# Forgetting attention followed by a SwiGLU block on one core: wider attention blocks, the decay inside the matmul, and the two stages interleaved

## The chip, the cores and the metric

The kernel runs on one core of a Trainium2 chip. The metric is the time of one execution on the device in microseconds. "The profile" is a record of one execution: which engine ran which instruction when, and what it had waited for. PE is the tensor engine, PEld its weight loads, ACT the scalar engine, DVE the vector engine, POOL GpSimd, SP the queue that issues most transfers.

## The reference

There are 64 heads (8 batches of 8 heads), 576 positions of 64 numbers each. The rows of attention are then the 4608 tokens of a gated feed-forward block (FFN) of width 512 and inner width 1536.

```python
scores = scale * q @ k.transpose(0, 1, 3, 2)
cum = cumsum(log(clip(f, 1e-4, 1)), axis=-1)
scores = where(causal, -1e9, scores + cum[:, :, :, None] - cum[:, :, None, :])
attn = softmax(scores) @ v                    # 64 heads, 576 x 576, causal
x = attn.transpose(0, 2, 1, 3).reshape(4608, 512)
g = x @ w_gate                                # 512 x 1536
out = (g * sigmoid(g) * (x @ w_val)) @ w_out  # 1536 x 512
```

## The kernel before

Attention comes first, head by head, in blocks of 96 by 96. q and k are transposed on PE in pieces of 96 by 64, so scores contract over 64 rows.

```python
for bh in range(BH):
    ...                                   # q, k, v by GpSimd transfers, cast to bf16
    for c in range(NBLK):                 # 6 blocks of 96
        nc.tensor.transpose(tq, qn[:, c, :], idN)
        nc.scalar.activation(qTp[:, c * BLK : (c + 1) * BLK], tq, AF.Copy, scale=scale)
        nc.tensor.transpose(tk, kn[:, c, :], idN)
        nc.vector.tensor_copy(kTp[:, c * BLK : (c + 1) * BLK], tk)
    ...                                   # cum_bc: decay of the queries on all rows
    for qi in range(NBLK):
        for kj in range(qi + 1):
            nc.tensor.matmul(sp, kTp[:, kj block], qTp[:, qi block])
            nc.vector.tensor_add(spa, sp, cum_bc[:, qi block])
            nc.scalar.activation(pt, spa, AF.Exp, bias=ncum_col[:, kj : kj + 1])
            ...                           # kj == qi: times a triangle, on DVE
            nc.tensor.matmul(op, pt, vb[:, kj, :], start=(kj == 0), stop=(kj == qi))
        ...                               # divide by the sum, store to attn_x in DRAM
```

Only when all heads are stored are the FFN's weights loaded. The FFN then takes 9 tiles of 512 tokens; each loads its rows from DRAM, transposes them on PE and does 144 matmuls of 512 columns.

The softmax here doesn't subtract the row's maximum and nothing guards it: scores larger than these inputs give would overflow.

Of the kernel before, what the change touches and what calls it, by code (L numbers as in the profile page):

```python
# [8 lines left out]
F32 = mybir.dt.float32  # L9
BF16 = mybir.dt.bfloat16  # L10
AF = mybir.ActivationFunctionType


@with_exitstack
def kernel(
    ctx: ExitStack,
    tc: tile.TileContext,
    q: bass.AP,
    k: bass.AP,
    v: bass.AP,  # L20
    f: bass.AP,
    moe_w_gate: bass.AP,
    moe_w_val: bass.AP,
    moe_w_out: bass.AP,
    out: bass.AP,
):
    nc = tc.nc
    B, H, S, D = q.shape
    BH = B * H
    N_TOK, D_MODEL = out.shape  # L30
    D_FF = moe_w_gate.shape[1]
    assert D_MODEL == H * D
    scale = 1.0 / (D ** 0.5)

    BLK = 96
    NBLK = S // BLK
    assert NBLK * BLK == S

    x_dram = nc.dram_tensor("attn_x", (N_TOK, D_MODEL), F32, kind="Internal").ap()
    cum_dram = nc.dram_tensor("cum_f", (BH, S), F32, kind="Internal").ap()  # L40
    ncum_dram = nc.dram_tensor("ncum_f", (BH, S), F32, kind="Internal").ap()

    fflat = f.rearrange("b h s -> (b h) s")
# [4 lines left out]
    with tc.tile_pool(name="cum", bufs=1) as cp:  # L48
        lf = cp.tile([BH, S], F32)
        nc.sync.dma_start(out=lf, in_=fflat)  # L50
        nc.scalar.activation(lf, lf, AF.Ln)
        tmp = cp.tile([BH, S], F32)
        d = 1
        src = lf
        dst = tmp
        while d < S:
            nc.vector.tensor_copy(dst[:, :d], src[:, :d])
            nc.vector.tensor_add(dst[:, d:], src[:, d:], src[:, : S - d])  # L58
            src, dst = dst, src
            d *= 2  # L60
        nc.sync.dma_start(out=cum_dram, in_=src)
        nc.scalar.mul(dst, src, -1.0)
        nc.sync.dma_start(out=ncum_dram, in_=dst)

    consts = ctx.enter_context(tc.tile_pool(name="consts", bufs=1))
    tri = consts.tile([BLK, BLK], F32)
    make_upper_triangular(nc, tri[:, :], val=1.0, diag=True)
    idN = consts.tile([BLK, BLK], BF16)
    make_identity(nc, idN[:, :])

    with ExitStack() as actx:
        hp = actx.enter_context(tc.tile_pool(name="head", bufs=2))
        pp = actx.enter_context(tc.tile_pool(name="p", bufs=3))
        psum = actx.enter_context(tc.tile_pool(name="psum", bufs=3, space=bass.MemoryType.PSUM))
        opsum = actx.enter_context(tc.tile_pool(name="opsum", bufs=2, space=bass.MemoryType.PSUM))
        tpsum = actx.enter_context(tc.tile_pool(name="tpsum", bufs=1, space=bass.MemoryType.PSUM))

        for bh in range(BH):
            b = bh // H
            h = bh % H  # L80
            qn = hp.tile([BLK, NBLK, D], BF16)
            kn = hp.tile([BLK, NBLK, D], BF16)
            nc.gpsimd.dma_start(out=qn, in_=qf[bh].rearrange("(n p) d -> p n d", p=BLK))  # L83
            nc.gpsimd.dma_start(out=kn, in_=kf[bh].rearrange("(n p) d -> p n d", p=BLK))  # L84
            qTp = hp.tile([D, S], BF16)
            kTp = hp.tile([D, S], BF16)
            for c in range(NBLK):
                tq = tpsum.tile([D, BLK], BF16)
                nc.tensor.transpose(tq, qn[:, c, :], idN)  # L89
                nc.scalar.activation(qTp[:, c * BLK : (c + 1) * BLK], tq, AF.Copy,  # L90
                                     scale=scale)
                tk = tpsum.tile([D, BLK], BF16)
                nc.tensor.transpose(tk, kn[:, c, :], idN)  # L93
                nc.vector.tensor_copy(kTp[:, c * BLK : (c + 1) * BLK], tk)  # L94
            cum_bc = hp.tile([BLK, S], F32)
            nc.gpsimd.dma_start(out=cum_bc[:1, :], in_=cum_dram[bh : bh + 1, :])
            nc.gpsimd.partition_broadcast(cum_bc, cum_bc[:1, :])
            ncum_col = hp.tile([BLK, NBLK], F32)
            nc.gpsimd.dma_start(
                out=ncum_col, in_=ncum_dram[bh].rearrange("(n p) -> p n", p=BLK)  # L100
            )
            vb = hp.tile([BLK, NBLK, D + 1], BF16)
            nc.gpsimd.dma_start(
                out=vb[:, :, :D], in_=vf[bh].rearrange("(n p) d -> p n d", p=BLK)
            )
            nc.vector.memset(vb[:, :, D : D + 1], 1.0)

            for qi in range(NBLK):
                op = opsum.tile([BLK, D + 1], F32)
                for kj in range(qi + 1):  # L110
                    sp = psum.tile([BLK, BLK], F32)
                    nc.tensor.matmul(  # L112
                        sp,
                        kTp[:, kj * BLK : (kj + 1) * BLK],
                        qTp[:, qi * BLK : (qi + 1) * BLK],
                        start=True,
                        stop=True,
                    )
                    spa = pp.tile([BLK, BLK], F32)
                    nc.vector.tensor_add(spa, sp, cum_bc[:, qi * BLK : (qi + 1) * BLK])  # L120
                    pt = pp.tile([BLK, BLK], BF16)
                    if kj == qi:
                        ptf = pp.tile([BLK, BLK], F32)
                        nc.scalar.activation(ptf, spa, AF.Exp,  # L124
                                             bias=ncum_col[:, kj : kj + 1])
                        nc.vector.tensor_mul(pt, ptf, tri)  # L126
                    else:
                        nc.scalar.activation(pt, spa, AF.Exp,  # L128
                                             bias=ncum_col[:, kj : kj + 1])
                    nc.tensor.matmul(  # L130
                        op, pt, vb[:, kj, :], start=(kj == 0), stop=(kj == qi)
                    )
                recip = pp.tile([BLK, 1], F32)
                nc.vector.reciprocal(recip, op[:, D : D + 1])  # L134
                ot = pp.tile([BLK, D], F32)
                nc.scalar.activation(ot, op[:, :D], AF.Copy, scale=recip)  # L136
                nc.sync.dma_start(
                    out=x_dram[b * S + qi * BLK : b * S + (qi + 1) * BLK,
                               h * D : (h + 1) * D],
                    in_=ot,  # L140
                )

    P = 128
    MT = 512
    KD = D_MODEL // P
    KF = D_FF // P

    idP = consts.tile([P, P], BF16)
    make_identity(nc, idP[:, :])

    wpool = ctx.enter_context(tc.tile_pool(name="wpool", bufs=1))
    wg = wpool.tile([P, KD, D_FF], BF16)
    wv = wpool.tile([P, KD, D_FF], BF16)
    wo = wpool.tile([P, KF, D_MODEL], BF16)
    nc.gpsimd.dma_start(out=wg, in_=moe_w_gate.rearrange("(ko p) n -> p ko n", p=P))
    nc.gpsimd.dma_start(out=wv, in_=moe_w_val.rearrange("(ko p) n -> p ko n", p=P))
    nc.gpsimd.dma_start(out=wo, in_=moe_w_out.rearrange("(ko p) n -> p ko n", p=P))

    xp = ctx.enter_context(tc.tile_pool(name="xp", bufs=2))
    xtp = ctx.enter_context(tc.tile_pool(name="xtp", bufs=2))  # L160
    hpool = ctx.enter_context(tc.tile_pool(name="hp2", bufs=2))
    spool = ctx.enter_context(tc.tile_pool(name="sp2", bufs=3))
    fpsum = ctx.enter_context(tc.tile_pool(name="fpsum", bufs=2, space=bass.MemoryType.PSUM))
    ops = ctx.enter_context(tc.tile_pool(name="ops", bufs=2, space=bass.MemoryType.PSUM))
    tps2 = ctx.enter_context(tc.tile_pool(name="tps2", bufs=2, space=bass.MemoryType.PSUM))
    opool = ctx.enter_context(tc.tile_pool(name="opool", bufs=3))

    NMT = N_TOK // MT
    for mt in range(NMT):
        xt = xtp.tile([P, KD, MT], BF16)  # L170
        for ms in range(MT // P):
            xn = xp.tile([P, D_MODEL], BF16)
            nc.gpsimd.dma_start(  # L173
                out=xn, in_=x_dram[mt * MT + ms * P : mt * MT + (ms + 1) * P, :]
            )
            for ko in range(KD):
                tp = tps2.tile([P, P], BF16)
                nc.tensor.transpose(tp, xn[:, ko * P : (ko + 1) * P], idP)  # L178
                nc.vector.tensor_copy(xt[:, ko, ms * P : (ms + 1) * P], tp)  # L179
# [59 lines left out]
```

## Time and profile before

| | before |
|---|---|
| median of the first 5 runs | 1107.03 us (1106.3 to 1109.13) |
| busy: PE, ACT, DVE, POOL | 93%, 56%, 53%, 27% |
| attention, to about 740 us | 11.0 us a head |
| FFN, from about 770 us | about 39 us a tile |

The lines from which these come are shown in the prediction. A high busy share says only that some instruction was in the array; how many columns pass per microsecond has to be read from start to start.

### The profile page before, as it was taken

The numbers are of one execution on the slowest core, as the hardware profiler recorded it, in microseconds if no ns is written. First come the engines' busy times: TensorE is split into PE (matmuls) and PEld (weight loads), VectorE is DVE, ScalarE is ACT, GpSimd is POOL, SyncE is SP. The second block draws the span as 40 slices with busy tenths as digits, with TensorE's granted clock in tenths as the row PEclk, the third lists the DMA queues.
The fourth block names the chain that finished last, engine by engine and source line by source line (L and its number), as shares of the span: only waits on it lengthen the run. The fifth ranks groups of instructions, "written<-read, shape, count | busy, mean of one in ns | idle before, by whom it ended". The sixth has DMA issues, their size and how long they took to land.

```text
span 1104.2 us, 18439 instructions
## 1 busy us (share of the span) xinstructions
PE 1022.5 (93%) x4896; PEld 608.3 (55%) x4896; DVE 581.9 (53%) x2868; ACT 618.8 (56%) x2225; POOL 299.4 (27%) x433
## 2 busy tenths in 40 slices
PE   0899999999999999999999999977989889889888
PEld 0566666666666666666666666642434334334333
DVE  2566666666666666666666666652333333333333
ACT  1677777777777777777777777752112112202211
POOL 1443434343433333333343333320000000000000
PEclk9999999999999999999999999999999899889899
DMA  1543534343434444444444444338110220120111
GB/s 21 37 36 35 46 34 37 33 38 33 37 33 37 35 35 36 34 35 35 36 35 36 35 35 35 30 53 163 48 49 19 49 57 20 39 58 29 29 48 39
DMA packets 174090, 44.43 MB, mean 40 GB/s; under 512 B 162016, under 2 KB 168160, under 8 KB 173984
## 3 DMA queue, kind: packets, MB, share of 16 engines
q0 software_dynamic: 125552, 23.91, 27.3%
q1 hardware_dynamic: 48432, 19.34, 7.4%
q8 instruction: 38, 0.62, 0.2%
q14 instruction: 68, 0.56, 0.2%
HBM read 47.63 MB, written 19.17 MB: 60 GB/s over the span
## 4 chain that ended last, share of the span: by engine, by line
PE 72%; issue 19%; DMA 6%; DVE 1%; POOL 1%; ACT 0%; POOLq 0%; ACTq 0%
PE sp L112 26%; PE op L130 23%; PE tk L93 7%; PE tq L89 6%; DMA xn<-attn_x 5%; PE gp L185 3%; PE vp L190 3%; PE op L200 3%; PE tp L178 1%; DMA qn<-in_q_dram 0%; DVE xt L179 0%; DVE tmp L58 0%; DVE lf L58 0%; DMA lf<-in_f_dram 0%; DMA attn_x<-ot 0%
## 5 line engine op out<-in xcount | busy, mean ns | idle before, releaser
L112 PE MATMUL sp<-qTp,kTp 64*96 64x96 bf16 x1344 | 373.0, 306 | 1.9 <-DVE spa L120 1.9
L128 ACT ACTIVATE pt<-spa,ncum_col 96x96 bf16<-96x96 f32 x960 | 326.7, 367 | 47.0 <-PE op L130 39.9
L130 PE MATMUL op<-vb,pt 96*96 96x65 bf16 x1344 | 334.6, 285 | 0.4 <-ACT pt L128 0.2
L120 DVE TENSOR_TENSOR spa<-sp,cum_bc 96x96 f32<-96x96 f32 x1344 | 297.6, 244 | 19.0 <-ACT pt L128 14.3
L130 PEld LDWEIGHTS <-pt 96*96 96x96 bf16 x1344 | 188.2, 161 | 102.9 <-DVE pt L126 1.3
L112 PEld LDWEIGHTS <-kTp 64*96 64x96 bf16 x1344 | 190.2, 158 | 80.9 <-issue 3.2
L195 ACT ACTIVATE st<-gp 128x512 f32<-128x512 f32 x108 | 64.4, 597 | 271.0 <-PE gp L185 270.9
L124 ACT ACTIVATE ptf<-spa,ncum_col 96x96 f32<-96x96 f32 x384 | 139.8, 364 | 26.5 <-DVE spa L120 26.5
L196 DVE TENSOR_TENSOR hh<-st,vp 128x512 bf16<-128x512 f32 x108 | 74.3, 688 | 142.0 <-PE vp L190 142.0
L134 DVE RECIPROCAL recip<-op 96x1 f32<-96x1 f32 x384 | 62.9, 164 | 157.3 <-PE op L130 150.6
L89 PE MATMUL tq<-idN,qn 96*64 96x96 bf16 x384 | 108.8, 283 | 28.5 <-POOL idN masks.py:199 24.7
L185 PE MATMUL gp<-xt,wg 128*128 128x512 bf16 x432 | 123.6, 410 | 9.5 <-DMA wg<-in_moe_w_gate_dram 9.2
L136 ACT ACTIVATE ot<-op,recip 96x64 f32<-96x64 f32 x384 | 115.4, 301 | 29.5 <-DVE recip L134 24.6
L90 ACT ACTIVATE qTp<-tq 64x96 bf16<-64x96 bf16 x384 | 90.5, 236 | 70.5 <-PE tq L89 70.5
L94 DVE COPY kTp<-tk 64x96 bf16<-64x96 bf16 x384 | 75.3, 196 | 92.8 <-PE tk L93 92.5
L190 PE MATMUL vp<-xt,wv 128*128 128x512 bf16 x432 | 116.1, 393 | 1.9 <-DMA wv<-in_moe_w_val_dram 1.9
L93 PE MATMUL tk<-idN,kn 96*64 96x96 bf16 x384 | 110.0, 287 | 1.3 <-DVE kTp L94 0.9
L173 POOL DMA_DIRECT2D xn<-attn_x x36 | 19.2, 535 | 323.1 <-PE tp L178 316.9
L126 DVE TENSOR_TENSOR pt<-ptf,tri 96x96 bf16<-96x96 f32 x384 | 96.2, 250 | 3.2
L200 PE MATMUL op<-wo,hh 128*128 128x512 bf16 x432 | 94.7, 379 | 0.0
L83 POOL DMA_DIRECT2D qn<-in_q_dram x64 | 46.7, 729 | 173.5 <-PE op L130 155.2
L84 POOL DMA_DIRECT2D kn<-in_k_dram x64 | 46.8, 731 | 137.6 <-PE op L130 128.7
(36 smaller groups left out, 527.4 us busy)
## 6 DMA issues: line engine op xcount, KB each, us to landing
attn_x<-ot SPq DMA_DIRECT2D x384, 24.0 KB, 1.4
out_dram<-ot SPq DMA_DIRECT2D x36, 256.0 KB, 2.0
qn<-in_q_dram POOLq DMA_DIRECT2D x64, 72.0 KB, 2.9
kn<-in_k_dram POOLq DMA_DIRECT2D x64, 72.0 KB, 2.7
vb<-in_v_dram POOLq DMA_DIRECT2D x64, 72.0 KB, 2.9
xn<-attn_x POOLq DMA_DIRECT2D x36, 128.0 KB, 3.0
wg<-in_moe_w_gate_dram POOLq DMA_DIRECT2D x1, 1536.0 KB, 10.5
wv<-in_moe_w_val_dram POOLq DMA_DIRECT2D x1, 1536.0 KB, 17.2
```

Of the source, the lines that this page charges most:

```text
L89: nc.tensor.transpose(tq, qn[:, c, :], idN)
L93: nc.tensor.transpose(tk, kn[:, c, :], idN)
L112: nc.tensor.matmul(sp, kTp[:, kj * BLK : (kj + 1) * BLK], qTp[:, qi * BLK : (qi + 1) * BLK], start=True, stop=True,)
L120: nc.vector.tensor_add(spa, sp, cum_bc[:, qi * BLK : (qi + 1) * BLK])
L124: nc.scalar.activation(ptf, spa, AF.Exp, bias=ncum_col[:, kj : kj + 1])
L126: nc.vector.tensor_mul(pt, ptf, tri)
L128: nc.scalar.activation(pt, spa, AF.Exp, bias=ncum_col[:, kj : kj + 1])
L130: nc.tensor.matmul(op, pt, vb[:, kj, :], start=(kj == 0), stop=(kj == qi))
L136: nc.scalar.activation(ot, op[:, :D], AF.Copy, scale=recip)
L185: nc.tensor.matmul(gp, wg[:, ko, fc * P : (fc + 1) * P], xt[:, ko, :], start=(ko == 0), stop=(ko == KD - 1),)
L190: nc.tensor.matmul(vp, wv[:, ko, fc * P : (fc + 1) * P], xt[:, ko, :], start=(ko == 0), stop=(ko == KD - 1),)
L200: nc.tensor.matmul(op, hh[:, fc, ms * P : (ms + 1) * P], wo[:, fc, :], start=(fc == 0), stop=(fc == KF - 1),)
```

## The change

The intent is fewer and wider instructions in attention, no trip of its result through DRAM, and FFN work for PE while attention waits for other engines. The diff replaces nearly the whole body; this is its core, abridged.

```diff
-    BLK = 96 ... one head at a time, blocks of 96 x 96
+BANKS = [                       # (key block, first query, width), one PSUM bank each
+    [(0, 0, 256), (1, 128, 128)],
+    [(0, 256, 320), (3, 384, 192)],
+    [(1, 256, 320), (4, 512, 64)],
+    [(2, 256, 320)],
+]
+    KR = D + 4                  # 64 rows of q or k and four rows that carry the decay
+    def load(g):                # q, k, v of four heads as f32, 15 transfers
+        for nm, src in (("q", qf), ("k", kf), ("v", vf)):
+            for j in range(GH):
+                nc.sync.dma_start(out=t[:, : NB - 1, j, :],
+                    in_=src[g * GH + j, : (NB - 1) * P].rearrange("(n p) d -> p n d", p=P))
+            ...                 # one more for the last 64 positions
+    def stage(g):               # bf16 copies of q and k on ACT, v on POOL, decay rows:
+        nc.sync.dma_start(out=QT[b][D : D + 1], in_=cq[hs])
+        for r in range(3):
+            nc.sync.dma_start(out=KT[b][D + 1 + r : D + 2 + r, :, :S], in_=ck[hs, r])
+    def qk(self, i):            # scores with the decay, exp, triangle on POOL
+        nc.tensor.matmul(s[:, c : c + w], KT[...kt block], QT[...q0 : q0 + w])
+        nc.scalar.activation(self.pt[...], s[:, :c], AF.Exp, scale=0.125)
+        nc.gpsimd.affine_select(...)
+    def pv(self, i): ...        # values, transposed result; sums from columns of ones; ev on ACT
+    def collect(g, j):          # sums of a head into 32 partitions
+        nc.sync.dma_start(out=SC[g][...], in_=E[g, j][row : row + 1, :])
+    def recip(g):               # 1/sum, to DRAM, back on all rows
+        nc.vector.reciprocal(rc, SC.pop(g))
+        nc.sync.dma_start(out=rc_dram[g]..., in_=rc)
+        for a in range(2): nc.sync.dma_start(out=rb[...], in_=src[a]...to_broadcast(...))
+    def normalise(g): ...       # xT = ev * rb, the FFN's input, kept in SBUF
+    evp = tc.tile_pool(name="evp", bufs=5)
+    START = H + 3               # FFN units are spread among the heads from here on
+    want = max(0, (n_heads - START) * per_tile // H)
-            nc.scalar.activation(st, gp, AF.Silu)
+        nc.scalar.activation(th, g_, AF.Tanh, scale=0.5)   # silu from tanh
```

A scheduler orders the instructions of each engine at build time. So any edit can move others too.

## The prediction

> **What bounds the kernel now.** I read the page in this order: busy shares, slices, chain, groups, then windows and a timeline of one stretch. Shares and chain first:
>
> ```profile
> PE 1022.5 (93%) x4896; PEld 608.3 (55%) x4896; DVE 581.9 (53%) x2868; ACT 618.8 (56%) x2225; POOL 299.4 (27%) x433
> ...
> PE 72%; issue 19%; DMA 6%; DVE 1%; POOL 1%; ACT 0%; POOLq 0%; ACTq 0%
> ```
>
> The tensor engine (PE) is busy 93% and makes up most of the chain that ended last. But a busy PE is not a full one, so I ask what each matmul does:
>
> ```profile
> L112 PE MATMUL sp<-qTp,kTp 64*96 64x96 bf16 x1344 | 373.0, 306 | 1.9 <-DVE spa L120 1.9
> ...
> L130 PE MATMUL op<-vb,pt 96*96 96x65 bf16 x1344 | 334.6, 285 | 0.4 <-ACT pt L128 0.2
> ...
> L200 PE MATMUL op<-wo,hh 128*128 128x512 bf16 x432 | 94.7, 379 | 0.0
> ```
>
> A 96-column score matmul lasts 306 ns and a 512-column one 379 ns: a cost per instruction, hardly per column. The timeline shows which:
>
> ```profile
> 399.96 0.29 PE L130 MATMUL op<-vb,pt 96*96 96x65 bf16 x1
> ...
> 400.18 0.31 PE L112 MATMUL sp<-qTp,kTp 64*96 64x96 bf16 x1
> ...
> 400.42 0.29 PE L130 MATMUL op<-vb,pt 96*96 96x65 bf16 x1
> ...
> 401.08 0.39 PE L112 MATMUL sp<-qTp,kTp 64*96 64x96 bf16 x2
> ...
> 776.78 10.52 PE L200 MATMUL op<-wo,hh 128*128 128x512 bf16 x48
> ```
>
> Where kinds alternate, starts are 0.22 us apart; two of one kind fit in 0.39 us where one takes 0.31, so 0.08 us apart. I read that as a cost of about 0.14 us for changing the shape of the array in use (64 rows, 64 columns, full). It is an inference: a 96*96 `op` beside a 128*128 transpose, both full, follows in 0.10 us. The 48 matmuls of 512 columns run at (10.52-0.38)/47 = 0.216 us.
>
> ```profile
> 100.00:740.00 640.00, 637.20 (x3140) 422.55 (x3140) 409.01 (x2332) 496.68 (x1912) 246.18 (x344) 1.00 0.42 36
> 740.00:770.00 30.00, 17.66 (x71) 7.17 (x71) 5.93 (x14) 5.96 (x9) 3.62 (x5) 1.00 0.97 170
> ...
> 800.00:1104.00 304.00, 270.62 (x1216) 120.63 (x1214) 104.70 (x235) 53.74 (x90) 13.74 (x26) 0.93 0.16 39
> ```
>
> Columns: window, length, busy us of PE, weight load, DVE, ACT, POOL with counts, clock, DMA share, GB/s. So three stages: attention to about 740 us (21+21+12 = 54 matmuls a head in 640*54/3140 = 11.0 us), a hole of some 9 us for the weights, then the FFN, about 39 us a tile where 144 matmuls at 0.216 need 31. There PE stops at each tile for `xn` from DRAM and its clock dips (0.93).
>
> **What the Trainium skill says.** "TensorE: Matmul & The Clock Gate", Back-to-back issue gap, gives N/2.4 + 2.5 ns warm, 216 ns at 512 columns; the trace has 216. "ScalarE: Activation LUTs", What ACT_TABLE_LOAD costs, gives 186 + 0.833 N ns with immediate scale, less about 93 ns back to back; the trace has 597 ns at 512 (612 by the formula) and two in 1.08 us. The same page, Table sets, puts exp and tanh in one set, so tanh instead of Silu lets exp and FFN mix without reloads: the compiled change has two table loads, before has three of 1283 ns. "Perfetto Trace Analysis", Optimization Strategy, warns that consistent bubbles can mean too few buffers; I use that below.
>
> **The change part by part.** It is a rewrite, all of it counted from the compiled order of instructions.
>
> 1. Attention on PE. Blocks of 128 keys by up to 320 queries replace 96 by 96; only the causal part is computed. A head has 7 score matmuls (256, 128, 320, 192, 320, 64, 320 columns), 7 value matmuls of the same widths, and 5 transposes (10 for q and k of each pair of heads). By the gap formula, with 80 ns as the floor seen in pairs: 109+80+3*136+83+80 = 0.76 us, twice, 1.52 us. The transposes: four at about 0.13 us (pairs of 128-column `tp` take 0.35 against 0.22 for one), one of 64 rows at 0.1 plus two shape changes of 0.14: 0.9 us. Together 2.4 us against 11.0 now. The row count for scores is 68 (four rows carry the decay), which I take to run as the full shape.
> 2. The decay goes from DVE and ACT into the matmul: 1344 additions (298 us of DVE) and the per-column bias vanish. The sum over keys comes from columns of ones, 64 instead of one, free in the array.
> 3. ACT per head: four exps over 1600 columns, two evictions of 576, staging copies of 640 columns on average. At 0.83 ns plus some 75 ns each: 1.63+0.63+0.63 = 2.9 us; FFN share 1.0 us. POOL: 5 triangle masks at up to 0.29 us (the 128x128 `idP` select took 293 ns) and V copies, an estimate of 2 us. DVE: two transposed copies and one normalisation of 576 columns at 0.65 us, 1.5 FFN pairs of 1.25 us: 3.9 us.
> 4. FFN on PE is unchanged: 1296 matmuls * 0.216 = 280 us. But it is interleaved with attention from head 11 on: 53 heads get 2 units each (3.9 us), 38 units stay for the end. The order keeps 352 matmuls after the last attention: 76 us, plus about 3 for the last store. No `attn_x` round trip, no FFN transposes, no hole for weights.
> 5. Start. Q, K and V load as f32 on one SP queue, 256-byte runs: 6912 packets for four heads. Queue 1 in before took 7.4% of 16 engines for 48432 packets, 27 ns each, the software queue 38; at 30 ns a group costs 6912*30/16 = 13 us. The queue is in order, and the decay rows of group 0 stand behind the loads of groups 0 and 1: first score at about 2+26+3 = 31 us.
> 6. A first phase with no FFN. Each group's decay rows wait for the next group's loads. And there are five `ev` buffers for four heads a group: the second head of a group cannot evict until the group before is normalised, after gather DMA, reciprocal, write to DRAM, broadcast read. DMAs land in 1.4 to 2.9 us, and sit behind loads in the queue: I estimate 14 us. Group 0 takes 31 to 48, then periods of about 20 us with weights (25 us of full DMA) among them: head 11 done at about 93 us, of which PE needed 26.
>
> Sum: steady phase ideal 53*(2.4+3.9) = 334 us; bursts of two heads stall on exp, mask and `ev`, for which I add 6% (20 us): 354. Total 93+354+79 = 526 us. Cross-check: all PE work 64*2.4+280 = 434, plus 31 start, 36 lost in the first phase, 20 stalls, 3 end = 524. I predict 525 us, a ratio of 0.47.
>
> **The rivals.** (a) The normalisation chain becomes the bound: if the round trip takes 22 us and not 14, a group of four heads takes about 30 us (chain plus two heads with their FFN), 7.5 a head, and 53 heads 398: total 585 with a slower start. For it: in-order queue, five buffers. Against: the order puts some 15 us of FFN and attention between. (b) The small packets bind: 110592 at 40 ns over 16 engines are 276 us over the run, under the span, so only the first phase suffers, 20 us more. For it: 162016 packets under 512 B already cost 35% of 16 engines. (c) ACT binds at 3.9 us plus waits a head, against 6.3 on PE: only if a semaphore hop of 0.1 to 0.2 us stands before every exp; total up to 560. (d) PE packs better than I sum: transposes overlap and shape changes cost nothing, 5.7 us a head and a first phase of 75: 470. (e) The clock drops in the first phase, where PE would be under half busy: some 10 to 15 us. Not faster at all would need the interleave to lose all its overlap: 280 FFN plus 64 heads at over 12 us, which I see nothing for.
>
> **Range and chances.** (d) sets the low end, (a) the high end: 475 to 590. The gain comes from several independent places (attention PE work 700 to 154, the hole, the FFN's waits), so faster is near certain: 0.985; within 2% 0.01, slower 0.005.
>
> **What would show it.** Steps: score matmuls of mean spacing about 0.11 us; FFN ones 0.216; first score near 31 us and no FFN matmul before 80; PE busy over 90% from 100 us on, the last 76 us with FFN alone; clock near 1.00; ACT near 60 to 65% busy, DVE 60 to 65%, POOL under 40%. Wrong if PE idles in holes of several us each group before transposes or the evictions `ev`, with releasers among DMA `rb` or DVE `xT` (then a), if the first score comes after 45 us (then b), or if the exp group shows ACT solid through the middle (then c).

## The result, and the profile after

| | before | after |
|---|---|---|
| median | 1108.44 us (15 runs) | 519.88 us (8 runs, 518.02 to 520.49) |
| ratio | | 0.469, interval 0.4684 to 0.4695 |
| heads 1 to 12 done | | at 99.6 us (24 FFN matmuls before) |
| heads 13 to 64 | | 339.3 us, 6.53 us a head |
| from there to the end | | 79.8 us |

The result is correct. Ratios here are the mean time of one kernel's fast runs over that of the other's of the same rounds, so not quite the ratio of the medians quoted. The last three rows are read from the ends of the value matmuls in the trace of one run (span 518.7 us).

From the page of the changed kernel come busy time by engine and the granted clock in 40 slices (the share of PE's full clock, in tenths).

```profile
PE 445.9 (86%) x2512; PEld 228.1 (44%) x2512; DVE 263.4 (51%) x436; ACT 279.4 (54%) x595; POOL 133.8 (26%) x410
...
PEclk9975575899999999999999999999999998999999
```

PE has half the instructions and less than half the busy time. The clock is low in slices 3 to 8, about 26 to 104 us, and dips once more in slice 34, at about 430 us. The next view, busy time by window with the columns explained in the prediction, says the same.

```profile
0.00:35.00 35.00, 11.35 (x65) 6.92 (x66) 14.14 (x18) 18.21 (x33) 22.80 (x46) 0.97 0.69 157
35.00:60.00 25.00, 10.60 (x54) 6.17 (x53) 3.65 (x8) 7.79 (x20) 6.94 (x22) 0.50 1.08 196
60.00:100.00 40.00, 26.65 (x145) 14.48 (x142) 13.74 (x26) 20.43 (x47) 11.87 (x39) 0.65 0.71 117
100.00:200.00 100.00, 94.92 (x561) 48.79 (x560) 57.24 (x98) 62.39 (x136) 25.00 (x86) 1.00 0.53 107
```

In the first 100 us PE is busy 48.6; from then on it is about 95% busy, with 561 matmuls in 100 us against 491 before (3140 in 640), and most of them two to five times as wide. Matmuls also show a trap in the clock column: the views count a time for which the trace has no clock record as 1.00. The record begins at 29.8 us in the changed kernel, but only at 756.4 us in the kernel before, each time with a change to full clock. What held until then is read from the matmuls. These are eight FFN matmuls of 512 columns each in the kernel before, one set just before its record begins and one just after:

```profile
751.32 3.57 PE L185 MATMUL gp<-xt,wg 128*128 128x512 bf16 x8 [9.15 <-DMA wg<-in_moe_w_gate_dram]
...
758.43 1.90 PE L190 MATMUL vp<-xt,wv 128*128 128x512 bf16 x8 [1.86 <-DMA wv<-in_moe_w_val_dram]
```

They start about 0.43 us apart in the first set and 0.216 us apart in the second. Likewise a 128-column transpose of the FFN lasts 0.26 to 0.31 us among the last heads (727 to 742 us), and 0.22 us where full clock is recorded. No drop of the clock is recorded before 756.4 us. So, as far as instructions can be compared, the attention of the kernel before ran at half clock, although the prediction's window shows 1.00; and so did the first scores of the changed kernel, at 23.3 us. Part of the gain in attention is therefore clock. An estimate: in e_late below, attention alone at a recorded clock of 0.54 keeps PE busy 3.6 us a head (111.35 us for 586 matmuls, 19 a head) against 11.0 us before; at full clock it needs about 1.8 us. No run here raised the clock of the kernel before, so what that alone would give stays open.

The groups of the page:

```profile
L268 PE MATMUL gp<-xT,wg 128*128 128x512 bf16 x432 | 124.6, 385 | 3.1 <-DVE xT L257 2.7
...
L180 PE MATMUL s<-QT,KT 68*128 68x320 bf16 (+4 forms) x448 | 86.8, 278 | 24.8 <-DMA KT<-ck 12.6
...
L211 PE MATMUL o<-pt,VB 128*128 128x320 bf16 (+4 forms) x448 | 99.1, 277 | 4.4 <-POOL pt L196 1.8
...
L257 DVE TENSOR_TENSOR xT<-ev,rb 64x576 bf16<-64x576 f32 x64 | 46.6, 763 | 68.9 <-DMA rb<-rc_d 68.3
```

The score and value groups of before (`sp`, `op`: 1344 each, 708 us together) have become `s` and `o`: 448 each, 186 us. The FFN's matmuls are what they were. What is new is in the last row: DVE stood 68.3 us before `xT` until the broadcast `rb` of the reciprocals came back from DRAM. Where PE paid for that is in its timeline (start, duration, then in brackets the idle time before and what ended it):

```profile
23.34 0.91 PE L180 MATMUL s<-QT,KT 68*128 68x256 bf16 x4 [12.56 <-DMA KT<-ck]
...
59.76 0.74 PE L159 MATMUL tp<-ident,b_q 128*128 128x128 bf16 x5 [11.90 <-ACT ev L222]
61.84 0.58 PE L268 MATMUL gp<-xT,wg 128*128 128x512 bf16 x1 [0.62 <-DVE xT L257]
...
89.03 0.74 PE L159 MATMUL tp<-ident,b_q 128*128 128x128 bf16 x5 [9.95 <-ACT ev L222]
```

Three holes make up 34 us: one until the decay rows arrive, two in which a transpose waits for a PSUM buffer, whose eviction into `ev` waits for an `ev` buffer, which `xT` frees only when `rb` has come. DVE's timeline shows that round trip:

```profile
46.16 0.27 DVE L239 RECIPROCAL rc<-sc 128x18 f32<-128x18 f32 x1 [2.58 <-DMA sc<-ev]
58.50 1.42 DVE L257 TENSOR_TENSOR xT<-ev,rb 64x576 bf16<-64x576 f32 x2 [12.07 <-DMA rb<-rc_d]
...
77.56 0.27 DVE L239 RECIPROCAL rc<-sc 128x18 f32<-128x18 f32 x1 [4.17 <-DMA sc<-ev]
87.76 2.87 DVE L257 TENSOR_TENSOR xT<-ev,rb 64x576 bf16<-64x576 f32 x4 [9.94 <-DMA rb<-rc_d]
```

From reciprocal to `xT` is 12.3 us for the first group, 10.2 for the second, and 5.5 to 9.1 later, most often about 7.4. In the first stretch two weight transfers of 1.5 MB (11.3 and 11.8 us from issue to landing) and loads fill the 16 engines: the DMA share is 1.08. That these lengthen the round trip is likely, but no run here took the weights away.

### The profile page after: what moved, and what is told of

Its sections match the earlier page's. It is cut to its first block, busy times and chain, and to the rows that moved or that the text cites. A ratio compares the mean times of both kernels' runs of the same rounds, so it can differ in the third digit from the quotient of the medians.

```text
span 518.7 us, 7574 instructions
## 1 busy us (share of the span) xinstructions
PE 445.9 (86%) x2512; PEld 228.1 (44%) x2512; DVE 263.4 (51%) x436; ACT 279.4 (54%) x595; POOL 133.8 (26%) x410
## 3 DMA queue, kind: packets, MB, share of 16 engines
q1 hardware_dynamic: 130192, 47.95, 42.7%
## 4 chain that ended last, share of the span: by engine, by line
PE 60%; DVE 10%; DMA 9%; issue 7%; ACT 6%; SPq 6%; POOL 2%; ACTq 0%; DVEq 0%; POOLq 0%
PE fo L284 15%; PE gp L268 13%; PE vp L272 13%; PE o L211 9%; PE s L180 7%; DMA rb<-rc_d 4%; DVE xT L257 4%; SPq L80 3%; PE tp L159 3%; ACT pt L188 3%; DMA sc<-ev 3%; DVE QT L163 2%; POOL pt L196 2%; DVE KT L163 2%; DMA nat_q<-in_q_dram 2%
## 5 line engine op out<-in xcount | busy, mean ns | idle before, releaser
L196 POOL TENSOR_SCALAR_AFFINE_SELECT pt<-pt 128x128 bf16<-128x128 bf16 (+1 forms) x320 | 89.8, 298 | 291.5 <-ACT pt L188 286.3
L188 ACT ACTIVATE pt<-s 128x384 bf16<-128x384 f32 (+2 forms) x256 | 122.1, 510 | 31.8 <-PE s L180 29.6
L268 PE MATMUL gp<-xT,wg 128*128 128x512 bf16 x432 | 124.6, 385 | 3.1 <-DVE xT L257 2.7
L272 PE MATMUL vp<-xT,wv 128*128 128x512 bf16 x432 | 123.6, 384 | 1.5 <-DVE th L276 0.9
L275 ACT ACTIVATE th<-gp 128x512 f32<-128x512 f32 x108 | 64.5, 600 | 90.0 <-PE gp L268 88.8
L180 PE MATMUL s<-QT,KT 68*128 68x320 bf16 (+4 forms) x448 | 86.8, 278 | 24.8 <-DMA KT<-ck 12.6
L284 PE MATMUL fo<-wo,hh 128*128 128x512 bf16 x432 | 106.6, 379 | 1.3 <-DVE th L276 1.3
L211 PE MATMUL o<-pt,VB 128*128 128x320 bf16 (+4 forms) x448 | 99.1, 277 | 4.4 <-POOL pt L196 1.8
L276 DVE SCALAR_TENSOR_TENSOR th<-th,gp 128x512 f32<-128x512 f32 x108 | 73.5, 686 | 57.5 <-ACT th L275 56.9
L278 DVE TENSOR_TENSOR hh<-th,vp 128x512 bf16<-128x512 f32 x108 | 73.9, 686 | 20.3 <-PE vp L272 12.6
L257 DVE TENSOR_TENSOR xT<-ev,rb 64x576 bf16<-64x576 f32 x64 | 46.6, 763 | 68.9 <-DMA rb<-rc_d 68.3
## 6 DMA issues: line engine op xcount, KB each, us to landing
wg<-in_moe_w_gate_dram POOLq DMA_DIRECT2D x1, 1536.0 KB, 11.8
wv<-in_moe_w_val_dram POOLq DMA_DIRECT2D x1, 1536.0 KB, 11.3
```

Of the source, the lines that this page charges most:

```text
L180: nc.tensor.matmul(s[:, c : c + w], KT[self.b][:, self.j, kt * P : (kt + 1) * P], QT[self.b][:, self.j, q0 : q0 + w], start=True, stop=True,)
L188: nc.scalar.activation(self.pt[:, off : off + c], s[:, :c], AF.Exp, scale=0.125)
L196: nc.gpsimd.affine_select(out=self.pt[:, c : c + w], in_=self.pt[:, c : c + w], pattern=[[1, w]], compare_op=ALU.is_ge, fill=0.0, base=0, ...
L211: nc.tensor.matmul(o[:, q0 - q_lo : q0 - q_lo + w], VB[self.b][:, kt, self.j, :], self.pt[:, c : c + w], start=(i <= 1 and n == 0), stop=( ...
L257: nc.vector.tensor_mul(xT[a * D : (a + 1) * D, h // 2, b0 : b0 + S], e[a * D : (a + 1) * D], rb[a * D : (a + 1) * D, j // 2],)
L268: nc.tensor.matmul(g_, wg[:, ko, fc * P : (fc + 1) * P], xT[:, ko, t * MT : (t + 1) * MT], start=(ko == 0), stop=(ko == KD - 1))
```

## The experiments

The questions: is the matmul shape really what made attention slow before, what does the interleaving give, and where the 73 us come from by which the span exceeds PE's 445.9 us busy.

### Shape: two edits of the kernel before

**b_full.** The transposed copies of q and k live in 128-row buffers, zero below row 64, so that scores contract over the full array. The result is right.

```diff
+        qfull = [consts.tile([128, S], BF16, name=f"qfull{i}") for i in range(2)]   # kfull alike
+            nc.vector.memset(t[D:], 0.0)
-            qTp = hp.tile([D, S], BF16)
+            qTp = qfull[bh % 2]
-                nc.scalar.activation(qTp[:, ...], tq, AF.Copy, scale=scale)
+                nc.scalar.activation(qTp[:D, ...], tq, AF.Copy, scale=scale)
```

> The kernel before with q and k transposed into 128-row buffers whose rows 64 to 127 are zero, so that the score matmuls use the full array; nothing else. Theory S (alternating 64-row score and full value matmuls costs about 0.14 us at each switch, which is what PE spends in attention): alternating matmuls start about 0.10 us apart instead of 0.22, PE stops being the bound, ACT at 78% takes over, and the time falls by 100 to 160 us, to 950 to 1010. Rival D (the 0.22 us is the wait for data between the engines, or the weight load): within 1%.

Measured: 1021.6 us, ratio 0.9227 (0.9212 to 0.9241), 86 us less. PE's timeline of this run:

```profile
400.70 0.32 PE L117 MATMUL sp<-qfull,kfull 128*96 128x96 bf16 x1
400.81 0.27 PE L135 MATMUL op<-vb,pt 96*96 96x65 bf16 x1
...
402.04 0.29 PE L117 MATMUL sp<-qfull,kfull 128*96 128x96 bf16 x1
402.20 0.29 PE L135 MATMUL op<-vb,pt 96*96 96x65 bf16 x1
```

PE's order differs. A score matmul and a value matmul now start 0.11 and 0.16 us apart, where they were 0.22 apart. The direction is that of theory S, but the result is 12 us above its range: the transposes still use 64 columns and still alternate with the rest.

**b_full_all.** The transposes are made full as well: q and k are loaded into tiles of 128 columns with zeros in the upper 64.

```diff
+        qpad = [consts.tile([BLK, NBLK, 128], BF16, name=f"qpad{i}") for i in range(2)]   # kpad alike
+            nc.vector.memset(t[:, :, D:], 0.0)
-            qn = hp.tile([BLK, NBLK, D], BF16)
+            qn = qpad[bh % 2]
-            qTp = hp.tile([D, S], BF16)
+            qTp = hp.tile([128, S], BF16)
-                tq = tpsum.tile([D, BLK], BF16)
+                tq = tpsum.tile([128, BLK], BF16)
```

> The kernel before with the transposed copies of q and k padded to 128 columns as well, so that the transposes of q and k (now 96 by 128) and the score matmuls all use the full width of the array and no change of shape is left on the transposes' side. Right result. The run that padded the scores alone took 1021.6 us. Theory S (a change of the shape in use costs about 0.14 us at each change): twelve transposes a head change shape less often, so 30 to 60 us less than 1021.6, 960 to 990 us, unless the scalar engine, 88% busy there, holds it up. Theory N (padding helped for another reason, such as the weights' load): within 10 us of 1021.6.

Measured: 956.92 us, ratio 0.8645, another 65 us less, slightly more than the 30 to 60 expected. PE's order differs here too. Its timeline:

```profile
399.77 0.29 PE L135 MATMUL op<-vb,pt 96*96 96x65 bf16 x1
399.87 0.29 PE L117 MATMUL sp<-qTp,kTp 128*96 128x96 bf16 x1
399.96 0.28 PE L94 MATMUL tq<-idN,qpad 96*128 96x96 bf16 x1
400.04 0.36 PE L117 MATMUL sp<-qTp,kTp 128*96 128x96 bf16 x2
```

Three kinds follow each other 0.08 to 0.10 us apart. The number of instructions is unchanged and each does more work, yet 150 us are gone: the cost lay in changing the used shape of the array. The Trainium skill, "TensorEngine Tiling (Array Packing)", Key Properties, says that changing the tiling mode drains the tensor engine; the trace agrees in direction, if a matmul of 64 rows or 64 columns counts as another mode, and puts about 0.12 us on it. The clock records of these two runs begin at 668.7 and 601.2 us, and FFN matmuls just before are 0.43 us apart in both (see the trap above), so this is the cost at half clock. Both kernels are then no longer bound by PE alone: from 100 to 500 us PE is busy 94% and 92%, ACT 88% and 95%.

### The interleaving

**e_late.** The FFN's units are all put after the last head in the program. PE's order changes, by intent.

```diff
-    START = H + 3
+    START = BH + 1
```

> The changed kernel with the FFN held back until 65 heads are counted, so that nearly all heads run without FFN work between them. Theory A: the round trip of some 20 us plus two heads of some 9 us sets a group's period without FFN, 27 us as in the first phase, so the overlap is worth much: 650 to 720 us. Rival C (heads without FFN cost ACT's 3.3 us each, 64*3.3 + 280 + 23): 515 to 540 us, which would make the interleave worth nothing.

Measured: 607.86 us, ratio 0.5487, 88 us more. It lies between the two theories, because the scheduler still pulled some FFN work forward (PE was busy 91 of the 100 us up to 200 us). From 200 to 360 us it had none left. Windows, then DVE's timeline, of this run:

```profile
200.00:360.00 160.00, 111.35 (x586) 66.81 (x584) 50.72 (x98) 93.76 (x215) 54.17 (x187) 0.54 0.56 110
```

```profile
277.20 2.88 DVE L257 TENSOR_TENSOR xT<-ev,rb 64x576 bf16<-64x576 f32 x4 [6.97 <-DMA rb<-rc_d]
297.81 2.89 DVE L257 TENSOR_TENSOR xT<-ev,rb 64x576 bf16<-64x576 f32 x4 [6.87 <-DMA rb<-rc_d]
```

Attention alone goes in groups of four heads about every 20.6 us, 5.2 us a head, at half the clock. Of such a period some 7.3 us pass from reciprocal to `xT`; the rest is mostly the two heads that cannot evict before it. So the loop through the round trip bounds attention when nothing is put between. In the changed kernel a head with its share of the FFN, 3.8 us of PE work, takes 6.53 us: some 1.3 us more for 3.8 us of work.

**e_ev7.** Seven `ev` buffers instead of five, to let the next group evict while the last one waits; `rb` has one buffer instead of two to make room.

```diff
-    evp = ctx.enter_context(tc.tile_pool(name="evp", bufs=5))
+    evp = ctx.enter_context(tc.tile_pool(name="evp", bufs=7))
+    rbp = ctx.enter_context(tc.tile_pool(name="rbp", bufs=1))
-        rb = rp.tile([P, GH // 2, S], F32, name="rb", tag="rb")
+        rb = rbp.tile([P, GH // 2, S], F32, name="rb", tag="rb")
```

> The changed kernel with seven ev buffers instead of five (the broadcast tile rb gets one buffer instead of two to make room). Theory A (the first phase is bound by the normalisation round trip, because the second head of a group has no buffer to evict into): the two holes of 11.9 and 10.0 us before the transposes at 59.8 and 89.0 us shrink to under 3 us each, the clock stays up between 35 and 100 us, and the time falls by 20 to 30 us, to 490 to 500. In the steady phase no change. Rival B (the DMA engines, at a share of 1.08 from 35 to 60 us, are the bound there, and the wait only moves to the loads): under 8 us.

Measured: 543.99 us, ratio 0.4914: 24 us slower, a clear miss. The second hole is gone, the first is smaller, but the clock now dips all along (page and PE timeline of this run):

```profile
PEclk9965566999899989998799979998999789999999
```

```profile
57.00 0.75 PE L160 MATMUL tp<-ident,b_k 128*128 128x128 bf16 x5 [8.71 <-ACT ev L223]
```

In PE's order, some three heads of attention (runs of 53 matmuls) now stand together with no FFN between, where the changed kernel has at most 10 in a row after its first twelve heads, and output matmuls come in runs of up to 48. I take it that with five buffers the scheduler could not run that far ahead, so that the shortage of buffers acted as a governor of the interleaving; that is argued, not shown. Because three things changed (`ev`, `rb` and the order), this run doesn't measure what buffers alone would be worth.

### The round trip of the reciprocals

**e_nochain.** The gather, the write and the broadcast are taken out, and `xT` is a product of two operands that are there (the result is wrong). The work of PE, ACT and DVE hardly changes, but PE's order does: the first FFN matmul comes at 48.8 us, not 61.8.

```diff
     def collect(g, j):
+        return
     def recip(g):
-        ...                                  # reciprocal, store, two broadcasts
+        RB[g] = None
     def normalise(g):
-                rb[a * D : (a + 1) * D, j // 2],
+                e[a * D : (a + 1) * D],
```

> Wrong result on purpose: no gather of the sums, no reciprocal, no write to DRAM, no broadcast read; the normalisation multiplies ev by itself, so DVE does the same work. It bounds what the round trip costs in all. Theory A: 25 to 40 us less (the two holes and the clock of the first phase, and a few us of the 32 us of stalls in the steady phase): 480 to 495. Rival B (loads bind): under 10 us less.

Measured: 496.51 us, ratio 0.4483, 23.4 us less; just above the expected range. One window of this run, against 26.65 us of PE in the changed kernel (the clocks, 0.96 and 0.65, can't be compared: this run's record begins at 68.9 us, and its FFN matmuls last 0.63 us until then, as at half clock):

```profile
60.00:100.00 40.00, 32.90 (x200) 18.55 (x205) 21.30 (x36) 26.50 (x61) 16.47 (x49) 0.96 0.93 169
```

Twelve heads are done at 92.2 us, with 37 FFN matmuls on record (a few are missing) instead of 24. That is 7.4 us plus 13 * 0.216 = 2.8 us, so some 10 us of the gain fall in the first phase and the other 13 later. The first phase stays slow: PE waits 8.5 us for loads of k and 6.5 us for a weight. So taking the chain out, with the order that comes with it, removes the two holes before transposes of 11.90 and 9.95 us, but transfers leave holes of 8.5 and 6.5 us without it.

**e_chainact.** The gather is issued from ACT, which wrote `ev`, not from SP, where loads stand ahead.

```diff
-        nc.sync.dma_start(
+        nc.scalar.dma_start(
             out=SC[g][j * n : (j + 1) * n, :], in_=E[g, j][row : row + 1, :]
```

> The changed kernel with the gather of the sums (sc<-ev, 64 transfers) issued from the scalar engine, which wrote ev, instead of the SP queue, where it stands behind loads. Right result. Theory A (the round trip behind loads in the in-order queue costs the time): the two holes of 11.9 and 10.0 us of the first phase shrink by some 3 to 5 us each, total 500 to 515 us. Theory O (what counts is the order that the scheduler picks; the edit also changes it): total within 6 us of 519.9 or above it, with holes moved elsewhere.[...]

Measured: 515.71 us (513.19 to 517.5), ratio 0.4664 (0.4653 to 0.4675), about 4 us less. The trace is of the fastest run, 513.19 us. In it the first hole before a transpose is 12.5 us and not shorter; the second is 5.9 us instead of 9.95, as theory A has it. Yet twelve heads are done at 99.8 us; the gain lies in the later heads (331.6 us for 52 against 339.3). An issue takes 0.51 us on ACT, 33 us for all 64. PE's order differs, too. So the first phase gained nothing on balance, and what the later gain is owed to, queue or order, stays open.

### The start and the loads

SP's queue at the start of the changed kernel (start, duration of the issue):

```profile
10.30 2.25 SPq L80 DMA_DIRECT2D nat_q<-in_q_dram  x4
...
19.24 0.77 SPq L143 DMA_DIRECT2D QT<-cq  x1
```

A load takes 0.56 us to issue, and 30 of them stand before the decay rows, which were computed by 15.6 us.

**e_ck0.** The four transfers of the decay rows of group 0 are issued from ACT. PE's order is the same to the instruction.

```diff
-        nc.sync.dma_start(out=QT[b][D : D + 1], in_=cq[hs])
+        (nc.scalar if g == 0 else nc.sync).dma_start(out=QT[b][D : D + 1], in_=cq[hs])
         # the three rows of KT alike
```

> The changed kernel with the four transfers of the decay rows of group 0 alone issued from the scalar engine instead of the SP queue, where they stand behind 30 loads. Right result, and the tensor engine's order is the same to the instruction. The prediction's step 5 (the first score waits on those rows for the sake of the loads ahead of them): the last piece of ck is written at 15.6 us, so the first score comes at 17.5 to 19.5 us instead of 23.3. If the start is on the path the total falls by 3 to 5 us, 515 to 517; if the first hole (a wait on the sums of group 0 and the loads of group 1) takes it back, the total stays within 2 us of 519.9.

Measured: 519.93 us (516.72 to 521.18), ratio 0.47: no gain. PE's timeline:

```profile
18.46 0.91 PE L180 MATMUL s<-QT,KT 68*128 68x256 bf16 x4 [7.55 <-DMA nat_k<-in_k_dram]
...
58.74 0.75 PE L159 MATMUL tp<-ident,b_q 128*128 128x128 bf16 x5 [12.06 <-ACT ev L222]
...
62.47 0.63 PE L272 MATMUL vp<-xT,wv 128*128 128x512 bf16 x1
62.90 0.63 PE L268 MATMUL gp<-xT,wg 128*128 128x512 bf16 x1
```

The first score comes 4.9 us earlier, as expected, but the end of the first hole moves from 59.76 to 58.74 only. The start is not on the path; the round trip of group 0 takes most of it back. The trace is of the fastest of the four runs, 516.72 us, where the second hole is shorter too (7.4 us), so it shows more gain than the median has. (The bracket of the first line names a load as the last event; the last decay row was issued from 15.7 to 16.2 us.) The last two lines matter for the clock: the FFN matmuls are 0.43 us apart, as at half clock, and the windows view counts 1.00 there, since this run's record begins at 64.9 us.

**e_run1k.** Loads read 1024 bytes at a time from DRAM (a wrong order of rows; PE's order is the same).

```diff
-                    in_=src[...].rearrange("(n p) d -> p n d", p=P),
+                    in_=src[...].rearrange("(p n) d -> p n d", p=P),
```

> The changed kernel with q, k and v read in runs of 1024 bytes instead of 256 (another order of the rows, so a wrong result on purpose; same bytes, same number of transfers, the order on the tensor engine is the same to the instruction). Rival b of the prediction (small packets cost the start and the first phase): packets of queue 1 fall from 130 thousand to about 47 thousand, the first score comes 3 us or more earlier, the total is 10 to 20 us less, 500 to 510 us. Theory A (the start is bound by the issue of some 40 transfers at 0.56 us on one queue, and the first phase by the round trip of the reciprocals): first score within 2 us of 23.3, total within 6 us of 519.9.

Measured: 522.45 us, ratio 0.4718, 2.6 us more than the changed kernel. A load takes 0.66 us to issue instead of 0.56, and the first score comes at 25.7 us, 2.4 us later and so outside theory A's mark. This run doesn't test what it was meant to test: the staging tile still holds each head's 256 bytes apart, and the page still counts 130192 packets on queue 1. **e_run1k2** lays the tile out with heads outermost, so that both sides have 1024 bytes in a row; ACT's copies undo it.

```diff
-            t = natp.tile([P, NB, GH, D], F32, ...)
+            t = natp.tile([P, GH, NB, D], F32, ...)
-                    out=t[:, : NB - 1, j, :],
+                    out=t[:, j, : NB - 1, :],
+                    # and in_ as in e_run1k
```

> The run before of this name without the 2 changed the order in DRAM alone and left the packets at 130 thousand, since the pieces in SBUF were still 256 bytes; here the staging tiles are laid out so that both sides have runs of 1024 bytes (wrong order of rows, so a wrong result on purpose; same bytes and number of transfers; the order on the tensor engine is the same up to head 6 and differs a little after). Rival b (small packets cost the start and the first phase): packets of queue 1 fall below 60 thousand, the first score comes 3 us or more before 23.3, and the hole before the transposes of group 1 in the first phase shrinks by 4 us or more; total 495 to 510 us. Theory A (issue and waits of the queue, not packets): first score within 2 us of 23.3, first hole within 3 us of 11.9, total within 8 us of 519.9.

Measured: 510.56 us (510.07 to 511.44), ratio 0.4615, 9 us less. The page's row for the queue, of the changed kernel and then of e_run1k2 (packets, MB, share of the 16 engines):

```profile
q1 hardware_dynamic: 130192, 47.95, 42.7%
```

```profile
q1 hardware_dynamic: 56464, 47.95, 33.4%
```

By the total both theories miss, each by about 1 us. Theory A's marks for the start and the first hole hold and rival b's don't: the first score comes 1.4 us earlier (issue 0.50 us a load), the first hole is 11.1 us, twelve heads are done at 98.9 us. So packets bind neither start nor first phase. But the later 52 heads take 329.7 us instead of 339.3. PE's order differs after head 6, much as in e_chainact, which gained 7.7 us there, in its fastest run, with small packets; so this gain can't be put down to the packets.

**v_cast.** q, k and v come over GpSimd's software queue, q and k cast on the way: no staging copies on ACT, an SP queue with no loads, three staging buffers. PE's order differs.

```diff
-                nc.sync.dma_start(out=t[:, : NB - 1, j, :], ...)
+                nc.gpsimd.dma_start(out=t[:, : NB - 1, j, :], ...)    # t in bf16 for q and k
-            nc.scalar.copy(t[:, : NB - 1], src[:, : NB - 1])          # and its rest
```

> The changed kernel with q, k and v loaded on GpSimd's software queue, q and k cast to bf16 on the way, so that 64 staging copies leave the scalar engine, the SP queue holds only the sums and the decay rows, and three staging buffers fit instead of two. Right result. Theory A: the first score comes later or equal[...], the holes of the first phase vanish, steady phase closer to 5.9 us a head; 480 to 505 us. Rival: the issue of 240 transfers on GpSimd[...] stands before the triangle masks in that engine's order and stalls exps and value matmuls: 530 to 580 us.

Measured: 581.79 us, ratio 0.5255: the rival, a little beyond its range. PE's waits in this run (total, times, longest):

```profile
PE o L207 <- POOL pt L192: 52.2, 24, 12.1
```

Value matmuls wait 52 us for triangle masks. Loads cost GpSimd 0.77 us each to issue, and these issues alone (`nat_q`, `nat_k`, `nat_v` of line 80) make up about 19% of the chain that ended last in this run; the masks stand behind them in the same engine's order. Part of it is not issue time: before loads of `nat_q` GpSimd stood 70 us waiting for PE (41.4 for transposes, 28.5 for value matmuls).

### Versions meant to be faster

**v_ck0chain** joins e_ck0 and e_chainact; **v_ck0chain_h2** also sets START to H + 2. Both results are right.

> Both moves to the scalar engine's queue at once: decay rows of group 0, and the gather of the sums (which alone gave 515.7 us). Right result. If the gains add: 509 to 513 us. If the order of the scheduler (which begins the FFN inside group 1 here, while its data comes at the earliest after group 1's normalisation) decides: 515 to 530.

Measured: 518.82 us, ratio 0.4687. The gains do not add. PE's order differs: the scheduler put FFN matmuls ahead of attention in group 1, and PE stood waiting for their data.

```profile
59.56 0.59 PE L268 MATMUL gp<-xT,wg 128*128 128x512 bf16 x1 [15.50 <-DVE xT L257]
```

> The same with the FFN allowed one head earlier (START from H+3 to H+2), so that two more of its units may be spread among attention and two fewer stay for the end. Right result. Theory A (more overlap, fewer units at the end): 3 to 8 us under the run without it. Theory O (the order decides): within 4 us of it, either way.

PE's order changes, by intent. Measured: 514.44 us (512.3 to 516.01), ratio 0.4646 (0.4632 to 0.466): 4.4 us under the one without it, which theory A takes in by a hair and theory O misses by as little, and 1% under the changed kernel. It is the fastest correct version found, level with e_chainact within the spread. By the mark of 2% used here it is the same as the changed kernel.

## Why the prediction was right, by its own steps

The total was 525 against 519.88, but several parts are off and partly cancel, so that so close a hit is in part luck. In the profiled run the parts are 99.6 + 339.3 + 79.8 = 518.7; predicted were 93 + 354 + 79 = 526.

- **The reading of before (shape).** Confirmed: without shape changes the kernel before takes 150 us less with the same number of instructions. The inferred 0.14 us is 0.12 by the spacing in b_full_all. The 0.08 us within a pair was misread: in the trace the two score matmuls at 401.08 start 0.116 us apart (0.39 is where the second ends, and it lasts only 0.28). And the window's clock of 1.00 was taken at its word, while the matmuls show half clock.
- **Step 1, attention on PE, 2.4 us a head.** Too high by about 0.6. Five transposes took 0.45 us from the first start to the next matmul, not 0.9. This is PE's timeline of the changed kernel:

```profile
204.84 0.52 PE L159 MATMUL tp<-ident,b_k 128*128 128x128 bf16 x5
205.29 0.82 PE L268 MATMUL gp<-xT,wg 128*128 128x512 bf16 x3
```

  The shape changes at the 64-row piece do show in the single starts (medians at full clock): full pieces are 0.055 us apart, but the 64-row piece starts 0.15 us after the one before it, and the next matmul 0.13 us after it. So a change costs about 0.10 us, not 0.14, and the term most over-sized is the full pieces, 0.13 us each: that came from pairs of `tp` before which PE waits for the eviction `xt`, while the first pair of a tile, with no such wait, is 0.06 us apart (820.51 us). The floor of 80 ns is not there at full clock either: after 128 columns the next matmul starts 0.055 us later, after 64 columns 0.028. The seven scores need 0.68 us and the seven values 0.69, so a head needs 1.37 + 0.45 = 1.82 us.

- **Steps 2 and 3, the other engines.** ACT was expected at 60 to 65% and is at 62.4% from 100 to 200 us; POOL was expected under 40% and is at 25%. DVE was expected at 60 to 65% and is at 57%: a transposed copy of 576 columns takes 0.45 us, not 0.65.
- **Step 4, the FFN.** 0.216 us a matmul holds. The tail is 79.8 us against 79. No FFN matmul was to come before 80 us, but the first is at 61.84: the scheduler lifted some ahead, which I had not read from the order.
- **Step 5, first score at 31 us.** It came at 23.3. I had sized a group's loads by packets, 13 us. They take 8.9 us, the time to issue 15 loads on SP; the packets run beside. The 27 ns is a mean over the run; in this stretch a packet takes about 18 ns, so 6912 of them keep 16 engines busy 7.8 us. The queue behind which the decay rows stand is as I said (e_ck0), but it does not matter for the end.
- **Step 6, the first phase.** Expected 62 us from the first score to twelve heads done, measured 76. The mechanism is as stated, five `ev` buffers and the round trip behind them; but the trip is longer when all engines move data (12.3 us from reciprocal to `xT` in the first group against about 7.4 later). So the late start was over-sized and the first phase under-sized, by 8 and 14 us.
- **The stalls of the later phase, 20 us.** Mis-sized: with 52 * 1.82 = 95 us of attention and 920 FFN matmuls, 199 us, PE needs 294 of the 339 us; 45 are lost. These 25 us more and the 0.58 us a head less for attention (30 us) nearly cancel.
- **The rivals.** (a) is the right mechanism for the holes, worth 23.4 us in all (e_nochain), not the 60 feared, because FFN work lies between; with none between (e_late), it binds at 5.2 us a head. (b) fell for the start and the first phase (e_run1k2). (c) fell: PE waited 4.9 us in all for exps before scores. (d) has PE's need about right, 5.7 us a head against 1.82 + 3.8, though the changes of shape are not free and its shorter first phase did not come. Its 470 doesn't follow from its parts: 53 * 5.7 + 75 + 79 is 456, or 476 with the 20 us of stalls. (e) came in form: the recorded clock was 0.50 from 35 to 60 us. The Trainium skill, "TensorE: Matmul & The Clock Gate", HAM oscillation, says that idle gaps over some 3.4 us bring half the clock. The trace agrees only in part: the clock stayed at half through the holes of 11.90 and 9.95 us, but it had fallen at 33.2 and 74.2 us, before them, in stretches at full clock whose longest recorded wait was 0.65 us. What the half clock cost is not shown. That one of the eight runs has a mean clock of 0.98 and the others about 0.94, with the same times, settles nothing, since a record that begins later shows a higher mean (e_ck0: 0.973).

What stays open: what the kernel before would take at full clock, what the half clock of the first phase cost, whether later weights would shorten the first round trip, and how much of the later gain in e_run1k2 and e_chainact is owed to the order alone.

## What to carry to other kernels

Read from start to start, not from the busy share, what a small matmul costs, and pad shapes until neighbours agree before counting columns. Read the clock from the spacing of one known matmul as well, since a clock of 1.00 can mean that nothing was recorded. When a chain of transfers bounds a stage, put independent work of the bounding engine between; here that hid all but 23 us. With a scheduler that orders at build time, look at the order after each edit: seven `ev` buffers, with the order that came with them, made this kernel slower, and an earlier start or a freer queue won nothing where a later wait ended last.

## What the Trainium skill lacked or had wrong

- "TensorEngine Tiling (Array Packing)", Key Properties, has the drain but no time and does not say that plain matmuls of different row or column counts pay it: here starts 0.22 us apart instead of about 0.10 at half clock, 150 us of 1107. A 64-row transpose among 128-row ones pays about 0.10 us at full clock on each side of it (0.15 us after the piece before, where full pieces are 0.055 apart); scores of 68 rows beside values of 128 pay nothing (0.14 us from start to start at 320 columns).
- No page says that a clock record can begin late, at the first change to full clock, and that the time before it has to be read from the matmuls: in the kernel before it begins at 756.4 us, and matmuls of 512 columns start 0.43 us apart until then and 0.216 us apart after.
- "DMA: Bandwidth & Descriptors", Issuing engines are not separate DMA queues, calls the time to initiate a transfer usually small beside the transfer. For loads of 512 pieces of 256 bytes it was 0.56 us each on SP, 0.77 us on GpSimd, and these issues one after another take the 8.9 us in which a group of 15 loads is started.
